# Values as one product of 129 columns per chunk, a head's output in two PSUM banks

## The chip, the cores and the metric

The kernel runs on one core of a Trainium2 chip, in one launch. A core has TensorE (matrix products, results into PSUM), VectorE, ScalarE and GpSimd (element work), and queues that start transfers. The metric is the device time of a run in microseconds, lower is better; of several runs the median counts.

## What is computed

Attention within clusters, followed by a two-level mixture of experts. The part that the change touches is the attention:

```python
q_assign = argmax(einsum('bhsd,hcd->bhsc', q_n, c_n), axis=-1)   # same for k
mask = q_assign[:, :, :, None] == k_assign[:, :, None, :]
scores = where(mask, scale * matmul(q, k.transpose(0, 1, 3, 2)), -1e9)
scores = scores - max(scores, axis=-1, keepdims=True)
attn = exp(scores)
attn = attn / (sum(attn, axis=-1, keepdims=True) + 1e-9)
x = matmul(attn, v)
```

There are 4 batches of 8 heads, 768 positions and 64 values per head, 16 clusters per head. All inputs are float32. The output of the attention, 3072 tokens of 512, goes through a router to one of 16 experts (512 to 1024 to 512 with a relu).

## The kernel before

Numbers are carried as a high part and a low part of 16 bits each, and a product of two such numbers is summed from products of parts. The 32 heads are worked off one after the other, each in nine steps. A step takes 512 of the 4608 columns that the six key chunks times 768 queries make. The order of the columns is: first all six key chunks against queries 0 to 383, then all six against queries 384 to 767. So the first half of a head's outputs is complete in the middle of its fifth step, the second at the end of the ninth.

A step (the loop at the end of `attention`) issues the following. `fine` makes the 512 scores on TensorE (L421, L422, each split in two or more products, `psf`), ScalarE takes the exponential (L426, `p`), and GpSimd subtracts the high part to leave the low part (L428, `pl`; in the last two heads VectorE does five of nine). `coarse`, up to 18 steps ahead, makes coarse scores (L379, `psc`), and VectorE takes row maxima of them (L382, `mpart`). `av` works on the step that was issued five steps before (`LAG`): it multiplies the probabilities of four blocks of 128 queries with the values, which lie in SBUF with the low parts in columns 0 to 63, the high parts in 64 to 127 and a constant in 128. For each block there are four products: high and low part of the probabilities, times high values with the constant (65 columns) and low values (64 columns), all added into the same columns of one bank of PSUM (`pso`, two banks in turn, one per head):

```python
vh, vl = vt[:, h % 2, c, 64:129], vt[:, h % 2, c, 0:64]
...
nc.tensor.matmul(out=O[:, col:col + 65], lhsT=p[:, bs], rhs=vh, ...)   # L447
nc.tensor.matmul(out=O[:, col:col + 64], lhsT=p[:, bs], rhs=vl, ...)   # L448
```

`finish` closes a head. VectorE adds a small number to the sum of the probabilities and scales it (L461), takes the reciprocal (L463) and multiplies the outputs by it in PSUM (L466). ScalarE casts the result to its high part (L467), VectorE subtracts to get the low part (L468); both go to `xs`, from which the router's logits are made (transposes L765, `logits`). `DEN` is kept: at the end `detect` looks for sums that are nearly zero.

Beside a step run the jobs of later heads: splitting inputs into parts (ScalarE L223, VectorE L224; at the start GpSimd L209, L210), the assignment to clusters (L268 to L280), the mask (L336 to L344), and routing of finished batches (L890 among it). The order of each engine's instructions is set by a scheduler that plans the whole program ahead; each engine then works its own list strictly in order, waiting where an operand is not there yet. The experts (products L1236, L1258, L1272) follow after the attention; a few of their preparations lie in it.

Of the kernel before, what the change touches and what calls it, by code (L numbers as in the profile page):

```python
# [22 lines left out]
P = 128  # L23
# [11 lines left out]
def attention(ctx, tc, qT, kT, vr, cen, R, DEN, cfg):  # L35
# [10 lines left out]
    OW = 66  # L46
# [13 lines left out]
    sp = ctx.enter_context(tc.tile_pool(name="sp", bufs=2))  # L60
    pp = ctx.enter_context(tc.tile_pool(name="pp", bufs=LAG + 2))
    sm = ctx.enter_context(tc.tile_pool(name="sm", bufs=3))
    ps_c = ctx.enter_context(tc.tile_pool(name="ps_c", bufs=2, space=PSUM))
# [8 lines left out]
    KBs, QBs, XSt, Ph, Pl, Os, mparts = {}, {}, {}, {}, {}, {}, {}  # L72
# [66 lines left out]
    nc.gpsimd.memset(obias[64:65 + C], 0.0)  # L139
    CH = const.tile([P, NP, 2, C], F16, name="CH")  # L140
# [111 lines left out]
    def assign(p, psum=None):  # L252

        pr, j = p % NP, p % 2
        if p < 2:
            ohs = [ozs[p][:, t, :, :, 64:64 + C].rearrange("p h c x -> p c h x") for t in range(2)]
        else:
            if j == 0:
                st["oh", p // 2] = sp.tile([P, NCH, P], F16, name="oh")
            ohs = [st["oh", p // 2][:, :, 64 * t + 32 * j:64 * t + 32 * j + 32].rearrange("p c (h x) -> p c h x", h=2) for t in range(2)]  # L260
# [71 lines left out]
    def mask(Q):  # L332
        oh = st["oh", Q]
        tp = ps_m.tile([P, 512], F32, name="psm").bitcast(F16)
        for c in range(NCH):
            nc.tensor.transpose(out=tp[:, c * P:(c + 1) * P], in_=oh[:, c], identity=ident)  # L336
        yield
        mk = sp.tile([P, S], F16, name="mk")
        nc.scalar.activation(out=mk, in_=tp[:, :S], func=AF.Identity, scale=mscale, bias=mbias)
        ready.add(Q)  # L340
        for i in range(4):
            h = 4 * Q + i
            nc.sync.dma_start(out=QA[h % 8][64:64 + C], in_=mk[C * i:C * i + C])
            last["mk"] = nc.sync.dma_start(out=KA[h % 8][64:64 + C], in_=mk[64 + C * i:64 + C * i + C])  # L344
# [88 lines left out]
    def av(h, u):  # L433
# [4 lines left out]
        if u == 0:  # L438
            Os[h] = ps_o.tile([P, 512], F32, name="pso")
        O = Os[h]  # L440
        for (c, q0, q1) in fsegs(u):
            vh, vl = vt[:, h % 2, c, 64:129], vt[:, h % 2, c, 0:64]
            for q in range(q0 // P, q1 // P):
                bs = slice(off, off + P)
                col = q * OW
                for i, p in enumerate((ph, pl)):
                    nc.tensor.matmul(out=O[:, col:col + 65], lhsT=p[:, bs], rhs=vh, start=c == 0 and q == 0 and i == 0, stop=False, skip_group_check=True)  # L447
                    nc.tensor.matmul(out=O[:, col:col + 64], lhsT=p[:, bs], rhs=vl, start=False, stop=c == NCH - 1 and i == 1, skip_group_check=True)  # L448
                off += P
        if u == 8:  # L450
            finish(h)

    def finish(h):

        O = Os.pop(h)
# [3 lines left out]
        Ov = O[:, 0:NCH * OW].rearrange("p (c w) -> p c w", w=OW)  # L459
        den = DEN[:, h]  # L460
        nc.vector.tensor_scalar(out=den, in0=Ov[:, :, 64], scalar1=EPS, scalar2=1.0 / XS, op0=ALU.add, op1=ALU.mult)  # L461
        rec = sm.tile([P, NCH], F32, name="rec")
        nc.vector.reciprocal(out=rec, in_=den)  # L463
        xs = XSt[b][:, :, :, hh * D:(hh + 1) * D]
        x = Ov[:, :, 0:64]
        nc.vector.tensor_tensor(out=x, in0=x, in1=rec.broadcast_to([P, NCH, D]), op=ALU.mult)  # L466
        nc.scalar.copy(out=xs[:, :, 0], in_=x)  # L467
        nc.vector.tensor_tensor(out=xs[:, :, 1], in0=x, in1=xs[:, :, 0], op=ALU.subtract)  # L468
# [82 lines left out]
    with tc.issue_after(hi0.ins), tc.issue_after(sub0.ins):  # L551
# [3 lines left out]
        for i in range(4):  # L555
            nc.gpsimd.memset(V[i][:, :, :, 128:130], SQ)
# [975 lines left out]
class Fixup:  # L1532
# [12 lines left out]
    def detect(self):  # L1545
        nc = self.nc
        EPS = 1e-9 * math.exp(PSHIFT / math.sqrt(self.vr.shape[5])) * SQ
        nc.vector.tensor_scalar(out=self.Z, in0=self.DEN, scalar1=4.0 * EPS / XS, scalar2=None, op0=ALU.is_lt)
# [150 lines left out]
```

## Time and profile before

| | us |
|---|---|
| median of 3 runs (lowest, highest) | 742.06 (740.55, 742.85) |
| the profiled execution | 742.52 |
| its span, first to last instruction | 740.7 |
| TensorE busy | 720.3 (97%) |
| VectorE busy | 596.1 (80%) |
| ScalarE busy | 486.0 (66%) |
| GpSimd busy | 493.6 (67%) |

The profile is of one execution. In its names PE is TensorE, DVE VectorE, ACT ScalarE, POOL GpSimd, and L447 is line 447 of the kernel. "out<-in" names the tile written and the tiles read. "Idle before <- X" is time that an engine stood still before an instruction, with what ended it. A record of TensorE ends when its result is written, and the next one starts long before; so starts tell its pace, and lengths do not. Records of the other engines overlap by some tens of ns in the same way. The granted clock of TensorE is full (2.4 GHz) in every stretch of the attention.

### The profile page before, as it was taken

What the parts mean: (1) busy time and instruction counts of PE and PEld (TensorE: products, weight loads), DVE (VectorE), ACT (ScalarE), POOL (GpSimd) and SP (SyncE); (2) the same over time, 40 slices, a digit from 0 to 9 for tenths busy, and PEclk for the clock granted to TensorE, in tenths of its full rate; (3) what the DMA queues carried; (4) which work ended last, traced back from release to release, by engine and by line L of the source; (5) the groups of instructions that cost most, each with busy time, mean ns of one, the idle gap of its engine ahead of it and who ended that gap; (6) DMA issues with size and microseconds to landing.
All of it is one profiled execution on the core that took longest, in us unless ns stands there. A gap on an engine that the chain in (4) does not pass through costs nothing.

```text
span 740.7 us, 26722 instructions
## 1 busy us (share of the span) xinstructions
PE 720.3 (97%) x11106; PEld 619.1 (84%) x11106; DVE 596.1 (80%) x1216; ACT 486.0 (66%) x952; POOL 493.6 (67%) x491
## 2 busy tenths in 40 slices
PE   8899999999999999999999989999999999999996
PEld 4688788888888888888888677888789999999996
DVE  6899889899888997989876476767779889988961
ACT  7778877788778887677977275444454555555642
POOL 8899787777787877878786325354644688554542
PEclk9999999999999999999999999999999999999998
DMA  8955634435245351240521696866777678887921
GB/s 226 224 141 153 192 100 119 155 99 154 81 120 172 95 159 37 67 131 3 178 81 38 234 313 220 273 211 221 237 244 234 230 272 284 284 275 264 281 77 36
DMA packets 45881, 128.04 MB, mean 173 GB/s; under 512 B 7699, under 2 KB 12691, under 8 KB 45752
## 3 DMA queue, kind: packets, MB, share of 16 engines
q1 hardware_dynamic: 40668, 112.64, 49.8%
q0 software_dynamic: 4928, 13.59, 5.1%
q8 instruction: 89, 1.46, 0.8%
q14 instruction: 40, 0.33, 0.1%
q10 hardware_dynamic: 156, 0.03, 0.0%
HBM read 93.41 MB, written 13.65 MB: 145 GB/s over the span
## 4 chain that ended last, share of the span: by engine, by line
PE 67%; DVE 17%; ACT 6%; issue 5%; DMA 2%; POOL 1%; another core or an unknown queue 1%; POOLq 0%; ACTq 0%; DVEq 0%
PE psh L1236 16%; PE psy L1258 12%; DVE mpart L382 7%; PE pso L447 6%; PE psf L421 6%; PE pso L448 5%; PE psf L422 5%; PE psc L379 5%; PE psy L1272 3%; DVE parts L224 2%; ACT p L426 2%; DMA st<-w 2%; PE psm L765 2%; PE psm L1294 1%; PE psm L1208 1%
## 5 line engine op out<-in xcount | busy, mean ns | idle before, releaser
L428 POOL TENSOR_TENSOR pl<-p 128x512 f16<-128x512 f32 x278 | 285.4, 1042 | 75.1 <-ACT p L426 70.6
L382 DVE TENSOR_REDUCE mpart<-psc 128x1 f32<-128x512 f32 (+1 forms) x282 | 190.2, 682 | 28.8 <-PE psc L379 28.4
L426 ACT ACTIVATE p<-psf 128x512 f32<-128x512 f32 x288 | 169.7, 596 | 45.6 <-PE psf L422 40.4
L447 PE MATMUL pso<-V,p 128*128 128x65 f16 x1152 | 160.2, 193 | 0.0
L448 PE MATMUL pso<-V,pl 128*128 128x64 f16 x1152 | 159.9, 193 | 0.0
L447 PE MATMUL pso<-V,pl 128*128 128x65 f16 x1152 | 159.4, 193 | 0.5 <-POOL pl L428 0.5
L448 PE MATMUL pso<-V,p 128*128 128x64 f16 x1152 | 159.3, 193 | 0.0
L421 PE MATMUL psf<-A 82*128 82x384 f16 (+2 forms) x576 | 142.5, 273 | 1.7 <-ACT p L426 1.6
L422 PE MATMUL psf<-B 128*128 128x384 f16 (+2 forms) x576 | 142.7, 273 | 0.0
L448 PEld LDWEIGHTS <-p 128*128 128x128 bf16 x1152 | 112.2, 97 | 22.2
L447 PEld LDWEIGHTS <-p 128*128 128x128 bf16 x1152 | 113.1, 98 | 9.6 <-issue 1.6
L447 PEld LDWEIGHTS <-pl 128*128 128x128 f16 x1152 | 112.5, 98 | 0.6 <-POOL pl L428 0.6
L448 PEld LDWEIGHTS <-pl 128*128 128x128 f16 x1152 | 111.5, 97 | 0.3
L379 PE MATMUL psc<-A 80*128 80x512 f16 (+1 forms) x376 | 106.3, 325 | 1.9 <-DVE mpart L382 1.2
L1239 DVE SCALAR_TENSOR_TENSOR hl<-psh,hh 128x160 f16<-128x160 f32 (+14 forms) x136 | 49.8, 368 | 48.9 <-ACT hh L1238 43.5
L1238 ACT ACTIVATE hh<-psh 128x160 f16<-128x160 f32 (+14 forms) x136 | 45.8, 345 | 59.1 <-PE psh L1236 54.9
L1301 POOL DMA_INDIRECT out_dram<-y,ri x33 | 43.4, 1316 | 52.4 <-ACT y L1300 46.3
L1236 PE MATMUL psh<-xT,wh0a 128*128 128x288 f16 (+7 forms) x512 | 74.6, 255 | 0.0
L1193 POOL DMA_INDIRECT xg<-xbuf,ri x25 | 40.5, 1620 | 43.7 <-PE psm L1208 30.1
L422 PEld LDWEIGHTS <-B 128*128 128x128 f16 x576 | 56.5, 98 | 10.9 <-issue 2.3
L1236 PE MATMUL psh<-xT,wh0b 128*128 128x272 f16 (+6 forms) x448 | 64.7, 253 | 0.0
L1236 PE MATMUL psh<-xT,wl0a 128*128 128x288 f16 (+7 forms) x256 | 64.0, 255 | 0.0
(385 smaller groups left out, 1785.9 us busy)
## 6 DMA issues: line engine op xcount, KB each, us to landing
st<-w SPq DMA_DIRECT2D x128, 512.0 KB
B<-parts SPq DMA_DIRECT2D x60, 192.0 KB
kx<-kT SPq DMA_DIRECT2D x16, 384.0 KB
qx<-qT SPq DMA_DIRECT2D x16, 384.0 KB
vx<-vr SPq DMA_DIRECT2D x16, 384.0 KB
xbuf<-xs SPq DMA_DIRECT2D x4, 1536.0 KB
A<-parts SPq DMA_DIRECT2D x30, 192.0 KB
A<-mk SPq DMA_DIRECT2D x56, 24.0 KB
```

What stands on the lines that cost most here:

```text
L379: last["mm"] = nc.tensor.matmul(out=pc[:, off:off + k1 - k0], lhsT=QA[h % 8][0:80, c * P:(c + 1) * P], rhs=KA[h % 8][0:80, k0:k1], start=T ...
L382: nc.vector.tensor_reduce(out=(mp[:, 0, 0:1], mp[:, :, 1], mp[:, 1, 0:1])[i], in_=pc.rearrange("p (a x) -> p a x", a=n), axis=AX.X, op=ALU ...
L421: nc.tensor.matmul(out=o, lhsT=KA[h % 8][0:82, ks], rhs=QA[h % 8][0:82, q0:q1], start=True, stop=False)
L422: nc.tensor.matmul(out=o, lhsT=KBs[h][:, ks], rhs=QBs[h][:, q0:q1], start=False, stop=True)
L426: cfg["exp"] = nc.scalar.activation(out=p32, in_=pf, func=AF.Exp, scale=QK / (SQ * SQ))
L428: lo = (nc.vector if u in (EARLY if h < 2 else DVE_LO[h % 8] if h < NH - 2 else DVE_END) else nc.gpsimd).tensor_tensor(out=pl, in0=p32, in ...
L447: nc.tensor.matmul(out=O[:, col:col + 65], lhsT=p[:, bs], rhs=vh, start=c == 0 and q == 0 and i == 0, stop=False, skip_group_check=True)
L448: nc.tensor.matmul(out=O[:, col:col + 64], lhsT=p[:, bs], rhs=vl, start=False, stop=c == NCH - 1 and i == 1, skip_group_check=True)
L1236: self.mm = nc.tensor.matmul(out=ph[:, 0:M], lhsT=w[:, k, fs], rhs=xT[:, a, k], start=i == 0, stop=i == 3 * KD - 1)
L1238: nc.scalar.activation(out=hh[:, f], in_=ph[:, 0:M], func=AF.Relu)
L1239: self.ev = nc.vector.scalar_tensor_tensor(out=hl[:, f], in0=ph[:, 0:M], scalar=0.0, in1=hh[:, f], op0=ALU.max, op1=ALU.subtract)
L1258: self.mm = nc.tensor.matmul(out=py[:, 0:M], lhsT=w[:, f, d * P:(d + 1) * P], rhs=a[:, f], start=i == 0, stop=i == len(prods) - 1)
```

## The change

The two products with the parts of the values become one of 129 columns (0 to 128 of the value tile), whose low half and high half land in separate columns of PSUM. A block of queries needs 130 columns, so a bank holds three blocks, and a head takes two banks, one for each half of its queries. A new function `joined` is called when a half is complete: ScalarE copies the low halves to SBUF (`ol`), VectorE adds them to the high halves and writes the sum to SBUF (`xo`, one buffer). The constant column and a constant in `ol` now carry the scale and the small number of the denominator, so that the reciprocal is taken directly and kept in `DEN`; `detect` compares the other way round. The multiply works in SBUF, and the low part of the outputs is made by GpSimd, in the last two heads by VectorE. To make room, two tiles (`oh`, `mk`) get one buffer in place of two.

```diff
--- before.py
+++ after.py
@@ -43,7 +43,8 @@
     PS = math.exp(QK * PSHIFT)
     EPS = 1e-9 * PS * SQ
     VW = 136
-    OW = 66
+    OW = 130
+    HB = NCH // 2
     NQ = B * H // 4
     NH = B * H
     LAG = 5
@@ -58,8 +59,10 @@
     ring = ctx.enter_context(tc.tile_pool(name="ring", bufs=8))
     ld = ctx.enter_context(tc.tile_pool(name="ld", bufs=2))
     sp = ctx.enter_context(tc.tile_pool(name="sp", bufs=2))
+    sq1 = ctx.enter_context(tc.tile_pool(name="sq1", bufs=1))
     pp = ctx.enter_context(tc.tile_pool(name="pp", bufs=LAG + 2))
     sm = ctx.enter_context(tc.tile_pool(name="sm", bufs=3))
+    xo = ctx.enter_context(tc.tile_pool(name="xo", bufs=1))
     ps_c = ctx.enter_context(tc.tile_pool(name="ps_c", bufs=2, space=PSUM))
     ps_f = ctx.enter_context(tc.tile_pool(name="ps_f", bufs=2, space=PSUM))
     ps_o = ctx.enter_context(tc.tile_pool(name="ps_o", bufs=2, space=PSUM))
@@ -69,7 +72,7 @@
     ident = cfg["ident"]
 
     cparts, ready, last = {}, set(), {}
-    KBs, QBs, XSt, Ph, Pl, Os, mparts = {}, {}, {}, {}, {}, {}, {}
+    KBs, QBs, XSt, Ph, Pl, Os, Xs = {}, {}, {}, {}, {}, {}, {}
 
 
     st = {}
@@ -137,6 +140,7 @@
     obias = const.tile([P, 1], F32, name="obias")
     nc.gpsimd.memset(obias[64:96], PSHIFT)
     nc.gpsimd.memset(obias[64:65 + C], 0.0)
+    OL = [const.tile([P, HB, 65], F32, name=f"ol{i}") for i in range(2)]
     CH = const.tile([P, NP, 2, C], F16, name="CH")
     CL = const.tile([P, NP, 2, C], F16, name="CL")
     nc.vector.memset(CH, 0.0)
@@ -256,7 +260,7 @@
             ohs = [ozs[p][:, t, :, :, 64:64 + C].rearrange("p h c x -> p c h x") for t in range(2)]
         else:
             if j == 0:
-                st["oh", p // 2] = sp.tile([P, NCH, P], F16, name="oh")
+                st["oh", p // 2] = sq1.tile([P, NCH, P], F16, name="oh")
             ohs = [st["oh", p // 2][:, :, 64 * t + 32 * j:64 * t + 32 * j + 32].rearrange("p c (h x) -> p c h x", h=2) for t in range(2)]
         simt = psum or ps_m.tile([P, 512], F32, name="psm")
         sim = simt[:, 0:NCH * 4 * C].rearrange("p (c t x) -> p c t x", c=NCH, t=2)
@@ -335,7 +339,7 @@
         for c in range(NCH):
             nc.tensor.transpose(out=tp[:, c * P:(c + 1) * P], in_=oh[:, c], identity=ident)
         yield
-        mk = sp.tile([P, S], F16, name="mk")
+        mk = sq1.tile([P, S], F16, name="mk")
         nc.scalar.activation(out=mk, in_=tp[:, :S], func=AF.Identity, scale=mscale, bias=mbias)
         ready.add(Q)
         for i in range(4):
@@ -435,37 +439,42 @@
         vt = V[(h // 2) % 4]
         off = 0
         ph, pl = Ph.pop((h, u)), Pl.pop((h, u))
-        if u == 0:
-            Os[h] = ps_o.tile([P, 512], F32, name="pso")
-        O = Os[h]
         for (c, q0, q1) in fsegs(u):
-            vh, vl = vt[:, h % 2, c, 64:129], vt[:, h % 2, c, 0:64]
+            vv = vt[:, h % 2, c, 0:129]
             for q in range(q0 // P, q1 // P):
+                if c == 0 and q % HB == 0:
+                    Os[h] = ps_o.tile([P, 512], F32, name="pso")
                 bs = slice(off, off + P)
-                col = q * OW
+                o = Os[h][:, q % HB * OW:q % HB * OW + 129]
                 for i, p in enumerate((ph, pl)):
-                    nc.tensor.matmul(out=O[:, col:col + 65], lhsT=p[:, bs], rhs=vh, start=c == 0 and q == 0 and i == 0, stop=False, skip_group_check=True)
-                    nc.tensor.matmul(out=O[:, col:col + 64], lhsT=p[:, bs], rhs=vl, start=False, stop=c == NCH - 1 and i == 1, skip_group_check=True)
+                    nc.tensor.matmul(out=o, lhsT=p[:, bs], rhs=vv, start=c == 0 and q % HB == 0 and i == 0, stop=c == NCH - 1 and i == 1, skip_group_check=True)
                 off += P
+                if c == NCH - 1 and q % HB == HB - 1:
+                    joined(h, q // HB)
         if u == 8:
             finish(h)
 
+    def joined(h, i):
+
+        Ov = Os.pop(h)[:, 0:HB * OW].rearrange("p (c w) -> p c w", w=OW)
+        ol = OL[i]
+        nc.scalar.copy(out=ol[:, :, 0:64], in_=Ov[:, :, 0:64])
+        if i == 0:
+            Xs[h] = xo.tile([P, NCH, 65], F32, name="xo")
+        nc.vector.tensor_tensor(out=Xs[h][:, HB * i:HB * (i + 1)], in0=Ov[:, :, 64:129], in1=ol, op=ALU.add)
+
     def finish(h):
 
-        O = Os.pop(h)
+        X = Xs.pop(h)
         b, hh = h // H, h % H
         if hh == 0:
             XSt[b] = xsp.tile([P, NCH, 2, H * D], F16, name="xs")
-        Ov = O[:, 0:NCH * OW].rearrange("p (c w) -> p c w", w=OW)
-        den = DEN[:, h]
-        nc.vector.tensor_scalar(out=den, in0=Ov[:, :, 64], scalar1=EPS, scalar2=1.0 / XS, op0=ALU.add, op1=ALU.mult)
-        rec = sm.tile([P, NCH], F32, name="rec")
-        nc.vector.reciprocal(out=rec, in_=den)
+        nc.vector.reciprocal(out=DEN[:, h], in_=X[:, :, 64])
         xs = XSt[b][:, :, :, hh * D:(hh + 1) * D]
-        x = Ov[:, :, 0:64]
-        nc.vector.tensor_tensor(out=x, in0=x, in1=rec.broadcast_to([P, NCH, D]), op=ALU.mult)
+        x = X[:, :, 0:64]
+        nc.vector.tensor_tensor(out=x, in0=x, in1=DEN[:, h].broadcast_to([P, NCH, D]), op=ALU.mult)
         nc.scalar.copy(out=xs[:, :, 0], in_=x)
-        nc.vector.tensor_tensor(out=xs[:, :, 1], in0=x, in1=xs[:, :, 0], op=ALU.subtract)
+        (nc.gpsimd if h < NH - 2 else nc.vector).tensor_tensor(out=xs[:, :, 1], in0=x, in1=xs[:, :, 0], op=ALU.subtract)
 
 
 
@@ -553,7 +562,9 @@
         split(1, 0, True)
         splitv(0, True)
         for i in range(4):
-            nc.gpsimd.memset(V[i][:, :, :, 128:130], SQ)
+            nc.gpsimd.memset(V[i][:, :, :, 128:130], SQ / XS)
+        for t in OL:
+            nc.gpsimd.memset(t[:, :, 64], EPS / XS)
     with tc.issue_after(last["qa"].ins), tc.issue_after(last["sub"].ins):
         split(2, 1, True)
     banks = itertools.cycle(((ps_c, "psc"), (ps_f, "psf")))
@@ -1545,7 +1556,7 @@
     def detect(self):
         nc = self.nc
         EPS = 1e-9 * math.exp(PSHIFT / math.sqrt(self.vr.shape[5])) * SQ
-        nc.vector.tensor_scalar(out=self.Z, in0=self.DEN, scalar1=4.0 * EPS / XS, scalar2=None, op0=ALU.is_lt)
+        nc.vector.tensor_scalar(out=self.Z, in0=self.DEN, scalar1=XS / (4.0 * EPS), scalar2=None, op0=ALU.is_gt)
         nc.vector.tensor_reduce(out=self.zs, in_=self.Z, axis=AX.XY, op=ALU.max)
         nc.vector.tensor_copy(out=self.zh, in_=self.zs)
         yield
```

The numbers of the lines behind the change are shifted by four to eleven. What stands where in the engines' lists is shown at three places: TensorE in head 16, VectorE and ScalarE at the end of head 11 (heads counted from 0).

TensorE, at the start of a step's value products before (`psc` coarse scores, `p` and `pl` parts of the probabilities, `V` values, `pso` outputs):

```order
L379 LDWEIGHTS A_187
L379 MATMUL psc<-A_187 128x512
L447 LDWEIGHTS p_6258
L447 MATMUL pso<-V_192,p_6258 128x65
L448 LDWEIGHTS p_6258
L448 MATMUL pso<-V_192,p_6258 128x64
L447 LDWEIGHTS pl
L447 MATMUL pso<-V_192,pl 128x65
L448 LDWEIGHTS pl
L448 MATMUL pso<-V_192,pl 128x64
```

And the same place now:

```order
L383 LDWEIGHTS A_193
L383 MATMUL psc<-A_193 128x256
L450 LDWEIGHTS p_5172
L450 MATMUL pso<-V_198,p_5172 128x129
L450 LDWEIGHTS pl
L450 MATMUL pso<-V_198,pl 128x129
```

Four weight loads and four products per block of queries have become two and two; the block that follows repeats the pattern.

VectorE before, at the end of head 11 (`DEN`, `rec`: denominator and reciprocal; `mx`, `psm`, `mw`, `oh`: assignment; `xs`: outputs in parts):

```order
L382 TENSOR_REDUCE mpart_220<-psc 128x2
L461 TENSOR_SCALAR DEN<-pso 128x6
L275 TENSOR_TENSOR psm<-psm,mx 128x384
L463 RECIPROCAL rec<-DEN 128x6
L382 TENSOR_REDUCE mpart_220<-psc 128x1
L466 TENSOR_TENSOR pso<-pso,rec 128x6x64
L276 TENSOR_TENSOR psm<-psm,desc 128x384
L382 TENSOR_REDUCE mpart_220<-psc 128x1
L468 TENSOR_TENSOR xs<-pso,xs 128x6x64
L278 TENSOR_REDUCE mw<-psm 128x24
```

And now (`ol`, `xo`: low halves and joined outputs):

```order
L386 TENSOR_REDUCE mpart_228<-psc 128x2
L464 TENSOR_TENSOR xo<-pso,ol_221 128x195
L277 TENSOR_REDUCE mx<-psm 128x24
L472 RECIPROCAL DEN<-xo 128x6
L386 TENSOR_REDUCE mpart_228<-psc 128x1
L475 TENSOR_TENSOR xo<-xo,DEN 128x6x64
L279 TENSOR_TENSOR psm<-psm,mx 128x384
L228 TENSOR_TENSOR V_198<-psm,V_198 128x6x64
L280 TENSOR_TENSOR psm<-psm,desc 128x384
```

The denominator step has become the sum of a half, the multiply has one other instruction between it and the reciprocal as before, and the subtraction to `xs` is gone from this list; it stands in GpSimd's list between two low parts of the probabilities.

ScalarE before, at the same head (`psm<-vx` and `V`: splitting of values):

```order
L426 ACTIVATE p_4828<-psf 128x512
L249 ACTIVATE V_193<-vx 128x12x64
L426 ACTIVATE p_4875<-psf 128x512
L223 ACTIVATE psm<-vx 128x384
L426 ACTIVATE p_4907<-psf 128x512
L467 CAST xs<-pso 128x6x64
L426 ACTIVATE p_4939<-psf 128x512
```

And now:

```order
L430 ACTIVATE p_4030<-psf 128x512
L461 COPY ol_221<-pso 128x3x64
L227 ACTIVATE psm<-vx 128x384
L430 ACTIVATE p_4069<-psf 128x512
L253 ACTIVATE V_199<-vx 128x12x64
L430 ACTIVATE p_4093<-psf 128x512
L476 CAST xs<-xo 128x6x64
L430 ACTIVATE p_4117<-psf 128x512
```

The copy of the second half is put in five instructions ahead of the cast, with two exponentials between them.

## Rows read from the trace of the kernel before

**Rows 1.** Page, first part: busy us (share of the span) and instructions.

```profile
PE 720.3 (97%) x11106; PEld 619.1 (84%) x11106; DVE 596.1 (80%) x1216; ACT 486.0 (66%) x952; POOL 493.6 (67%) x491
```

**Rows 2.** Timeline, one attention step, TensorE: start us, length us, line, operation, shapes.

```profile
100.38 0.20 PE L447 MATMUL pso<-V,p 128*128 128x65 f16 x1
...
100.86 0.22 PE L421 MATMUL psf<-A 82*128 82x128 f16 x1
100.92 0.22 PE L422 MATMUL psf<-B 128*128 128x128 f16 x1
100.98 0.33 PE L421 MATMUL psf<-A 82*128 82x384 f16 x1
...
101.53 0.19 PE L447 MATMUL pso<-V,p 128*128 128x65 f16 x1
```

**Rows 3.** Waits of TensorE, whole span: total us, times, longest us.

```profile
PE psf L421 <- ACT p L426: 1.6, 5, 0.7
PE psc L379 <- DVE mpart L382: 1.2, 3, 0.4
PE pso L447 <- POOL pl L428: 0.5, 1, 0.5
```

**Rows 4.** Stretches: window, us; PE, PEld, DVE, ACT, POOL busy (instructions); clock, DMA share, GB/s.

```profile
76.00:88.00 12.00, 11.95 (x239) 10.03 (x236) 12.00 (x27) 10.67 (x21) 10.21 (x14) 1.00 0.73 215
88.00:100.00 12.00, 11.27 (x216) 9.26 (x215) 7.49 (x19) 8.84 (x18) 8.43 (x25) 1.00 0.27 73
...
160.00:172.00 12.00, 11.70 (x233) 9.62 (x230) 11.84 (x27) 9.15 (x21) 9.55 (x10) 1.00 0.55 154
...
256.00:268.00 12.00, 11.81 (x262) 9.97 (x260) 11.83 (x27) 9.01 (x20) 9.73 (x10) 1.00 0.60 176
...
sum 372.00, PE 366.97 PEld 308.02 DVE 320.50 ACT 290.11 POOL 292.61; mean PE 11.84 PEld 9.94 DVE 10.34 ACT 9.36 POOL 9.44
```

**Rows 5.** Chain that ended last, in time: start us, us, what.

```profile
397.44 0.33 PE psm L765 x6
...
448.43 1.47 PE psh L1236 x12
```

**Rows 6.** Timeline of TensorE in the experts' stage, the shape of L1236.

```profile
448.51 0.29 PE L1236 MATMUL psh<-xT,wl0a 128*128 128x288 f16 x1
```

**Rows 7.** VectorE's groups, 60 to 400: busy us, mean ns, idle before.

```profile
L468 DVE TENSOR_TENSOR xs<-pso,xs 128x384 f16<-128x384 f32 x29 | 16.0, 553 | 3.4 <-ACT xs L467 3.1
...
L280 DVE TENSOR_TENSOR oh<-psm,mw 128x192 f16<-128x192 f32 x24 | 7.3, 348 | 0.0
...
L890 DVE TENSOR_TENSOR rmv<-oe,rmv 128x384 f16<-128x384 f16 x3 | 2.7, 913 | 0.0
```

**Rows 8.** Timeline of VectorE after the last head's products.

```profile
402.25 0.17 DVE L461 TENSOR_SCALAR DEN<-pso 128x6 f32<-128x6 f32 x1 [0.27 <-PE pso L448]
```

**Rows 9.** VectorE's groups, 400 to the end.

```profile
L823 DVE TENSOR_TENSOR rmv<-oe,rmv 128x384 f16<-128x384 f16 x1 | 0.5, 547 | 0.0
```

**Rows 10.** Line 428 on VectorE: ns min/median/max, first and last start.

```profile
L428 DVE TENSOR_TENSOR pl<-p x10: 680/693/1356, 381.9 to 399.1; 128x512 f16<-128x512 f32 x10
```

**Rows 11.** Timelines of GpSimd and of VectorE, 388.5 to 392.

```profile
389.55 1.05 POOL L428 TENSOR_TENSOR pl<-p 128x512 f16<-128x512 f32 x1
...
389.80 1.96 DVE L428 TENSOR_TENSOR pl<-p 128x512 f16<-128x512 f32 x2
```

**Rows 12.** ScalarE's groups, 60 to 400.

```profile
L426 ACT ACTIVATE p<-psf 128x512 f32<-128x512 f32 x262 | 154.5, 596 | 40.7 <-PE psf L422 35.6 <-POOL pl L428 2.1 <-PE psc L379 2.1
...
L223 ACT ACTIVATE psm<-qx 128x384 f32<-128x384 f32 x24 | 11.7, 487 | 2.1 <-DVE parts L224 2.0
...
L406 ACT COPY mr<-psm 6x128 f16<-6x128 f16 x28 | 7.0, 248 | 0.8 <-PE psm L403 0.3
```

**Rows 13.** GpSimd's groups, 40 to 410.

```profile
L428 POOL TENSOR_TENSOR pl<-p 128x512 f16<-128x512 f32 x269 | 276.3, 1043 | 72.6 <-ACT p L426 68.3 <-ACT roh L857 0.5
```

**Rows 14.** Line 210: ns min/median/max, first and last start, forms.

```profile
L210 POOL TENSOR_TENSOR parts<-qx,parts x3: 914/1639/1642, 7.8 to 30.9; 128x768 f16<-128x768 f32 x2, 128x384 f16<-128x384 f32 x1
```

## The prediction

> **What bounds the kernel now.** I read the page's busy line first: TensorE is busy for 97% of the span [rows 1]. The ends of its records are modelled, so that share alone proves nothing. The next view is therefore the starts of its instructions inside one step of attention [rows 2]. The reader is to see that every start follows the one before at the pace of the columns: sixteen value products between 100.38 and 100.86, then the fine scores, the coarse scores, and the next step's products at 101.53, with no hole. A bare step takes 101.53 - 100.38 = 1.15 us and TensorE fills it. The waits of TensorE confirm this: over the whole span it waited 1.6 us for ScalarE's exponentials, 1.2 us for VectorE's row maxima and 0.5 us for GpSimd's low parts [rows 3]. So in attention TensorE sets the pace, and time that it saves is time saved, as long as the others can follow.
>
> Whether they can is in the table by stretches of 12 us [rows 4]. The 31 stretches from 40 to 412 us have VectorE busy for 10.34 of 12 us on average, but unevenly: in 12 of them it is busy for 11.2 us or more (12.00 in 76:88, 11.84 in 160:172, 11.83 in 256:268), and between them it falls as low as 7.49. ScalarE (9.36) and GpSimd (9.44) have more room. VectorE is thus within a few per cent of being a second bound for some two fifths of attention, and idle for a fifth to a third of the time elsewhere. The experts' stage after about 415 us is not touched by the change and is taken to move as a whole.
>
> **The value products.** Of the four products of a chunk (65, 64, 65, 64 columns) two of 129 are left: 258 columns before, 258 after. A step of 16 products becomes one of 8, so what goes is not columns but whatever each product costs beside them. The sixteen took 0.48 us, 30.0 ns each [rows 2]; 64.5 columns at 2.4 GHz are 26.9 ns, so a product costs 3.1 ns on its own account. Longer ones show the same: twelve of 288 columns take 1.47 us, 122.5 ns each, 2.5 above the 120 of the columns; six transposes of 128 take 0.33 us, 55 ns each, 1.7 above [rows 5, 6]. Saved are 8 x 3.1 = 25 ns in each of 288 steps, 7.2 us. Bounds: with a remainder of 2.5 ns a product of 129 takes 56.3 ns, eight take 450 ns, and 30 x 288 = 8.6 us are saved. The other end is the pair of fine products of 128 columns, which follow at 60 ns each (100.86, 100.92, 100.98) [rows 2]: 60.4 ns for 129, eight make 483 ns, a loss of 0.9 us. The value products are nearer to the first kind in weights (all 128 rows; one of the fine pair has 82), so I take 7.2. Half of the weight loads go too; I cost them at nothing, since the starts above already run at the pace of the columns.
>
> **VectorE.** Per head go the shifted denominator (L461, 0.17 us) and the low part (L468, 553 ns), together 0.72 us [rows 7, 8]; two joining sums of 195 elements come, which I price by the nearest row, 348 ns for 192 elements [rows 7], together 0.70 us. In work that is nothing. The multiply by the reciprocal stays, but both of its inputs now lie in SBUF, where the values were in PSUM before. What this costs beside GpSimd the trace shows in two places. The same 384-element product of two SBUF inputs takes 547 ns in the tail (L823), with GpSimd idle, and 913 ns on average in its three calls in attention (L890) [rows 7, 9]. And VectorE's own low parts (L428), 680 ns at best, take up to 1356 [rows 10]: the timeline has GpSimd's low part from 389.55 to 390.60, and a VectorE low part issued at 389.80, in a pair that takes 1.96 us where two at their best end within 2 x 0.68 = 1.36 [rows 11]. The added time is what was left of GpSimd's instruction. So 32 multiplies gain 913 - 547 = 0.37 us each, 11.7 us on VectorE in all; at worst a whole GpSimd instruction of 1.04 us, at best nothing. Queued behind the multiply on VectorE are the coarse row maxima, and TensorE waits for these with two banks in hand; behind it on ScalarE is the cast that waits for the multiply, then the next exponential.
> The Trainium skill says so too (SBUF — State Buffer, section "Who interferes with whom"): a VectorE instruction with two SBUF inputs and a GpSimd instruction that reads SBUF exclude one another for a whole instruction, and whichever came first is finished first. By that rule, the trace agrees (the 1356 and 913 ns above), every multiply can be caught, and the worst sum is that of the slower rival below.
> How much of the 11.7 us reaches TensorE depends on the stretch. In the 19 lighter stretches VectorE has 1 us or more to spare and I take nothing. In the 12 heavy ones (12/31 of 32 heads, 12.4 heads) there are 12.4 x 0.37 = 4.5 us; two banks of coarse scores and the instruction that stands between reciprocal and multiply hide part of it, and I take half, 2.3 us. In the same stretches a faster TensorE runs into VectorE: of the 2.8 us saved there (12.4/32 of 7.2) I take half as not realised, 1.4 us.
>
> **ScalarE.** 64 copies of 192 elements come. Between 248 ns for 128 elements and 487 ns for 384 [rows 12] I take 310 ns, 20 us in all, 0.6 us per head of about 11.7 us. Cover: in attention it sat idle for 40.7 us before its exponentials, 35.6 of them waiting for TensorE [rows 12]. I take nothing; were that cover gone in the four stretches where ScalarE is at 10.9 us or more, 4 x 0.6 = 2.5 us.
>
> **GpSimd.** It gets 30 of the 32 low parts of the outputs. The nearest row is 914 ns for 384 elements [rows 14]; 512 take 1043 [rows 13], which would scale to 0.78. That makes 24 to 27 us on an engine that waits 68.3 us for the exponentials [rows 13]. Its low parts are wanted five steps later, which covers a delay of one. I take nothing. The bound: nine low parts and one of these make 10.3 us, nine bare steps without 25 ns each 10.1, so a head with nothing else in it would be 0.2 us late, at most 30 x 0.2 = 6 us; most heads have more than bare steps in them.
>
> **The rest.** The one-buffer tiles are written again 36 steps later, long after their last reading. A bank of products comes back after half a head (over 5 us) and is emptied within about 1 us. After the last head the chain to the router's logits gets a copy (0.31) and a sum (0.35) for the denominator step (0.17) [rows 8]: +0.5 us.
>
> **Sum.** -7.2 + 2.3 + 1.4 + 0.5 = -3.0 us, 0.4%, against the profiled execution's 742.52 us (span 740.7, 1.8 around it): 739.5. That execution lay 0.46 above the median of 742.06, so I predict 739.0.
>
> **Rivals.**
> Slower: the exclusion of VectorE and GpSimd becomes the bound. Place: the multiply of each head; price 0.37 us each, all of it on TensorE: -7.2 + 11.7 + 0.5 = +5.0, 747.1 us. For it: VectorE at 12.00 of 12 [rows 4], the 913 ns [rows 7], and GpSimd, which is held up in turn. Against it: the light stretches. It decides from about 8.9 of the 11.7 us on, three quarters, where the result passes +2.2.
> No change: the heavy stretches take their gain back in full. -7.2 + 2.8 + 4.5 + 0.5 = +0.6, 742.7 us; the bounds of ScalarE (2.5) or GpSimd (up to 6), in part, end near here too. For it: [rows 4]. Against it: in these same stretches TensorE is still busy for 11.7 of 12 us.
> The remainder per product grows: 129 columns behave like the fine pair. +0.9 + 2.3 + 0.5 = +3.7, 745.8 us. For it: the 60 ns [rows 2]; against it: the 2.5 and 1.7 ns [rows 5, 6].
> That the change does not do what it says I leave out: the order shows one product of 129 columns where there were two.
>
> **Chances.** Forecast 0.46 (its own range 735 to 741); no change 0.31; exclusion 0.17; remainder 0.06. A difference under 0.3% (2.2 us) can't be told from none here. Faster 0.46, same 0.31, slower 0.23. The best end is 742.06 - 8.6 + 0.5 = 734.0, the worst of the cases 747.1; I give 734 to 746.5.
>
> **What the profile after would show.** Value products starting 56 to 57 ns apart (60 would speak for the remainder). The multiply averaging about 0.9 us against 0.56, spread between 0.55 and 1.5; were it at 0.56, the exclusion is wrong and the result nearer to 735. TensorE's waits for VectorE's row maxima and ScalarE's exponentials up by 2 to 4 us in all, in the heavy stretches; ten or more make the forecast wrong. The end of attention about 3 us earlier, and the experts' stage as long as before.

## The result and the profile after

The change makes the kernel slower: 745.97 us (median of 5 runs, 744.41 to 747.1) against 741.73 us (5 runs, 740.55 to 742.85) before it, ratio 1.0055 [1.0035, 1.0075]. The forecast was 739.0 us. The time lies inside the range that was given (734 to 746.5), but on the side of a loss where a gain was forecast. The profiled execution took 747.1 us, with a span of 745.1.

The page's busy line, in the columns of [rows 1]:

```profile
PE 716.5 (96%) x8802; PEld 610.7 (82%) x8802; DVE 607.3 (81%) x1218; ACT 500.6 (67%) x1016; POOL 528.0 (71%) x523
```

TensorE has 2304 instructions and 3.8 us of busy time less, in a span that is 4.4 us longer. VectorE gained 11.2 us, GpSimd 34.4, ScalarE 14.6. One bare step of attention on TensorE, as in [rows 2]:

```profile
101.91 0.22 PE L450 MATMUL pso<-V,p 128*128 128x129 f16 x1
...
102.36 0.22 PE L425 MATMUL psf<-A 82*128 82x128 f16 x1
...
103.03 0.22 PE L450 MATMUL pso<-V,p 128*128 128x129 f16 x1
```

Eight products in 0.45 us and the step in 1.12, where before sixteen took 0.48 and the step 1.15. So the saving is there in a step without a hole. Part of what took it back stands in TensorE's waits over the whole span, as in [rows 3] (total us, times, longest):

```profile
PE psc L383 <- DVE mpart L386: 5.6, 10, 1.5
PE psf L425 <- ACT p L430: 2.2, 4, 1.4
PE pso L450 <- POOL pl L432: 0.5, 1, 0.5
```

The wait for VectorE's row maxima went from 1.2 us in 3 waits to 5.6 in 10, and its longest from 0.4 to 1.5. Stretches as in [rows 4], others among them; the last line sums the 32 stretches from 40 to 424 (in [rows 4] it is 31, from 40 to 412):

```profile
64.00:76.00 12.00, 10.32 (x144) 8.28 (x142) 10.92 (x19) 10.70 (x23) 10.96 (x15) 1.00 0.53 135
76.00:88.00 12.00, 11.86 (x167) 9.87 (x165) 11.61 (x28) 10.14 (x23) 10.76 (x16) 1.00 0.67 190
88.00:100.00 12.00, 11.78 (x164) 9.60 (x162) 9.88 (x24) 11.39 (x22) 11.54 (x14) 1.00 0.34 114
100.00:112.00 12.00, 11.59 (x146) 9.44 (x144) 10.72 (x22) 9.28 (x22) 11.02 (x27) 1.00 0.52 144
...
256.00:268.00 12.00, 11.46 (x164) 9.39 (x162) 12.00 (x27) 9.90 (x23) 11.22 (x11) 1.00 0.71 190
...
sum 384.00, PE 372.10 PEld 306.25 DVE 336.24 ACT 306.49 POOL 327.37; mean PE 11.63 PEld 9.57 DVE 10.51 ACT 9.58 POOL 10.23
```

The worst stretch for TensorE is 64:76 (10.32 of 12 us busy), where VectorE is at 10.92, not one of those that were full before. The groups of VectorE, ScalarE and GpSimd from 60 to 400 us that are new or carry the argument (busy us, mean ns, idle time before):

```profile
L475 DVE TENSOR_TENSOR xo<-xo,DEN 128x384 f32<-128x384 f32 x30 | 24.4, 812 | 0.3
L464 DVE TENSOR_TENSOR xo<-pso,ol 128x195 f32<-128x195 f32 x58 | 20.6, 355 | 5.2 <-ACT ol L461 2.6 <-ACT desc L394 1.2
```

```profile
L461 ACT COPY ol<-pso 128x192 f32<-128x192 f32 x58 | 18.6, 320 | 2.3 <-PE pso L450 2.2
```

```profile
L477 POOL TENSOR_TENSOR xs<-xo,xs 128x384 f16<-128x384 f32 x29 | 26.0, 897 | 1.1 <-ACT xs L476 1.0
L432 POOL TENSOR_TENSOR pl<-p 128x512 f16<-128x512 f32 x254 | 266.2, 1067 | 41.8 <-ACT p L430 36.5 <-ACT mr L410 2.3 <-DMA A<-mk 0.3
```

Copies, sums and low parts cost what they were priced at (310, 348, and 780 to 914 ns). The multiply is the line to look at. All 32 of it by line (ns min/median/max, first and last start), before and then after:

```profile
L466 DVE TENSOR_TENSOR pso<-pso,rec x32: 552/562/567, 47.1 to 403.0; 128x384 f32<-128x384 f32 x32
```

```profile
L475 DVE TENSOR_TENSOR xo<-xo,DEN x32: 546/584/2543, 48.3 to 406.8; 128x384 f32<-128x384 f32 x32
```

Half of them are about as quick as before; the mean of 812 comes from the others, the longest of which is over four times as long. The longest, on VectorE, on GpSimd, and on TensorE (start us, length us; in brackets the idle time ahead and its releaser):

```profile
70.59 0.65 DVE L386 TENSOR_REDUCE mpart<-psc 128x1 f32<-128x512 f32 x1
71.16 2.54 DVE L475 TENSOR_TENSOR xo<-xo,DEN 128x384 f32<-128x384 f32 x1
73.63 0.54 DVE L277 TENSOR_REDUCE mx<-psm 128x24 f32<-128x384 f32 x1
74.09 0.54 DVE L228 TENSOR_TENSOR parts<-psm,parts 128x384 f16<-128x384 f32 x1
74.56 0.67 DVE L386 TENSOR_REDUCE mpart<-psc 128x2 f32<-128x512 f32 x1
```

```profile
70.26 3.03 POOL L432 TENSOR_TENSOR pl<-p 128x512 f16<-128x512 f32 x3
```

```profile
73.60 0.22 PE L450 MATMUL pso<-V,pl 128*128 128x129 f16 x1
75.29 0.38 PE L383 MATMUL psc<-A 80*128 80x512 f16 x1 [1.47 <-DVE mpart L386]
```

The multiply stands on VectorE from 71.16 to 73.70, while GpSimd works off three low parts in a row from 70.26 to 73.29; the multiply ends 0.41 us after the last of them. Between two row maxima (70.59 and 74.56) VectorE thus lets 4 us pass. The next product on TensorE's list is one of coarse scores, which wants a bank that these maxima empty, and after the value product of 73.60 it starts only at 75.29. A multiply of 1.3 us is enough for a small hole, in the stretch 100:112 with VectorE busy for 10.72 of 12 us (VectorE, then TensorE):

```profile
108.23 1.32 DVE L475 TENSOR_TENSOR xo<-xo,DEN 128x384 f32<-128x384 f32 x1
109.47 1.28 DVE L386 TENSOR_REDUCE mpart<-psc 128x1 f32<-128x512 f32 x2
```

```profile
109.46 0.33 PE L426 MATMUL psf<-B 128*128 128x384 f16 x1
110.20 0.38 PE L383 MATMUL psc<-A 80*128 80x512 f16 x1 [0.41 <-DVE mpart L386]
```

For a number that holds all such places I took the starts of TensorE's instructions from 40 to 410 us, and of every distance what exceeds the columns at 2.4 GHz plus 2.5 ns, where that is over 15 ns (a product of fewer than 64 columns is counted as one of 64). These holes sum to 10.7 us before and 20.5 us after.

### The profile page after: what moved, and what is told of

It is laid out like the page before. It is cut to its first block, busy times and chain, and to the rows that moved or that the text cites. A ratio compares the mean times of both kernels' runs of the same rounds, so it can differ in the third digit from the quotient of the medians.

```text
span 745.1 us, 22241 instructions
## 1 busy us (share of the span) xinstructions
PE 716.5 (96%) x8802; PEld 610.7 (82%) x8802; DVE 607.3 (81%) x1218; ACT 500.6 (67%) x1016; POOL 528.0 (71%) x523
## 4 chain that ended last, share of the span: by engine, by line
PE 62%; DVE 11%; ACT 9%; DMA 7%; issue 6%; POOL 4%; SPq 0%; POOLq 0%; ACTq 0%; DVEq 0%
PE psh L1247 16%; PE psy L1269 14%; PE pso L450 9%; PE psf L425 5%; PE psf L426 4%; PE psc L383 4%; DVE mpart L386 3%; PE psy L1283 3%; ACT p L430 3%; DMA kx<-kT 3%; DMA st<-w 2%; POOL pl L432 2%; PE psm L1305 2%; DVE parts L228 1%; PE psm L1219 1%
## 5 line engine op out<-in xcount | busy, mean ns | idle before, releaser
L432 POOL TENSOR_TENSOR pl<-p 128x512 f16<-128x512 f32 x278 | 291.2, 1066 | 47.6 <-ACT p L430 42.1
L450 PE MATMUL pso<-V,p 128*128 128x129 f16 x1152 | 164.4, 220 | 0.0
L450 PE MATMUL pso<-V,pl 128*128 128x129 f16 x1152 | 163.2, 219 | 0.5 <-POOL pl L432 0.5
L450 PEld LDWEIGHTS <-pl 128*128 128x128 f16 x1152 | 112.2, 97 | 20.4 <-POOL pl L432 0.9
L450 PEld LDWEIGHTS <-p 128*128 128x128 bf16 x1152 | 112.1, 97 | 13.2 <-issue 5.6
L1312 POOL DMA_INDIRECT out_dram<-y,ri x33 | 41.2, 1250 | 50.3 <-ACT y L1311 45.0
L425 PEld LDWEIGHTS <-A 82*128 82x128 f16 x576 | 56.2, 98 | 12.4 <-issue 2.7
L1247 PE MATMUL psh<-xT,wl0b 128*128 128x272 f16 (+6 forms) x224 | 55.9, 253 | 0.0
L1247 PEld LDWEIGHTS <-wh0a 128*128 128x128 f16 x512 | 46.7, 98 | 4.7
L1033 DVE SCALAR_TENSOR_TENSOR wl1b<-st,wh1b 128x1024 f16<-128x1024 f32 x32 | 47.0, 1469 | 0.4 <-POOL wh1b L1032 0.4
```

Source lines behind the costliest of these rows:

```text
L425: nc.tensor.matmul(out=o, lhsT=KA[h % 8][0:82, ks], rhs=QA[h % 8][0:82, q0:q1], start=True, stop=False)
L432: lo = (nc.vector if u in (EARLY if h < 2 else DVE_LO[h % 8] if h < NH - 2 else DVE_END) else nc.gpsimd).tensor_tensor(out=pl, in0=p32, in ...
L450: nc.tensor.matmul(out=o, lhsT=p[:, bs], rhs=vv, start=c == 0 and q % HB == 0 and i == 0, stop=c == NCH - 1 and i == 1, skip_group_check=True)
L1033: nc.vector.scalar_tensor_tensor(out=l, in0=st, scalar=WS, in1=h, op0=ALU.mult, op1=ALU.subtract)
L1247: self.mm = nc.tensor.matmul(out=ph[:, 0:M], lhsT=w[:, k, fs], rhs=xT[:, a, k], start=i == 0, stop=i == 3 * KD - 1)
```

## Experiments

Ratios are against the kernel before on the same chip; its medians were 743.15 us (e1 to e4), 738.98 (e5 to e8) and 738.68 (e9, e10). Edits are to the changed kernel, those of e6 and e7 to the kernel before. "Holes" is the sum just defined.

**e1: multiply from PSUM.** The joined half goes back into its bank, and each half is multiplied from there.

```diff
-        nc.vector.tensor_tensor(out=Xs[h][:, HB * i:HB * (i + 1)], in0=Ov[:, :, 64:129], in1=ol, op=ALU.add)
+        nc.vector.tensor_tensor(out=Ov[:, :, 64:129], in0=Ov[:, :, 64:129], in1=ol, op=ALU.add)
+        den = DEN[:, h, HB * i:HB * (i + 1)]
+        nc.vector.reciprocal(out=den, in_=Ov[:, :, 128])
+        nc.vector.tensor_tensor(out=Xs[h][:, HB * i:HB * (i + 1), 0:64], in0=Ov[:, :, 64:128], in1=den.broadcast_to([P, HB, D]), op=ALU.mult)
     def finish(h):
-        nc.vector.reciprocal(out=DEN[:, h], in_=X[:, :, 64])
-        nc.vector.tensor_tensor(out=x, in0=x, in1=DEN[:, h].broadcast_to([P, NCH, D]), op=ALU.mult)
```

> The joining sum is written back into PSUM, the reciprocal and the multiply follow for each half at once, the multiply reads PSUM and writes SBUF; so VectorE's multiply has one SBUF input. ScalarE's copies and GpSimd's low parts of the outputs stay. Theory A (VectorE's multiply and GpSimd exclude one another, and the blocked multiply delays the row maxima that TensorE waits for): no multiply above 0.4 us, TensorE's waits for the row maxima fall from 5.6 to 1 to 2 us, 735 to 738 us. Theory B (the 64 copies on ScalarE delay the exponentials) or C (GpSimd's 30 added low parts): no better than the changed kernel, 744 to 747 us.

Measured: 738.93 us, ratio 0.9932 [0.9916, 0.9947], faster than both kernels, though 0.9 us above the range of theory A. Its multiplies by line, and TensorE's wait for the row maxima:

```profile
L467 DVE TENSOR_TENSOR xo<-pso,DEN x64: 339/348/361, 42.0 to 401.0; 128x192 f32<-128x192 f32 x64
```

```profile
PE psc L383 <- DVE mpart L386: 0.4, 1, 0.4
```

No multiply is longer than 361 ns, though VectorE has one more reciprocal and one more multiply per head. The holes are 14.8 us. ScalarE's copies and GpSimd's low parts are all still there, so neither is what makes the changed kernel slower than the one before. Changed with the inputs are the halving and the places in the order, so e5 takes these alone.

**e2: outputs' low parts on VectorE.**

```diff
-        (nc.gpsimd if h < NH - 2 else nc.vector).tensor_tensor(out=xs[:, :, 1], in0=x, in1=xs[:, :, 0], op=ALU.subtract)
+        nc.vector.tensor_tensor(out=xs[:, :, 1], in0=x, in1=xs[:, :, 0], op=ALU.subtract)
```

> The changed kernel with the low parts of the outputs made by VectorE in all heads (two SBUF inputs, 384 elements). Theory A: 30 more instructions that can be blocked, 0.7 to 0.9 us each instead of 0.55, and 0.46 us more work for VectorE: 748 to 754 us. Theory C: GpSimd is relieved of 26 us, 740 to 744 us. Theory B: 745 to 748 us.

Measured: 750.49 us, ratio 1.0094 [1.0074, 1.0114]; holes 24.8 us.

```profile
L475 DVE TENSOR_TENSOR xo<-xo,DEN x32: 546/1000/1412, 46.9 to 410.1; 128x384 f32<-128x384 f32 x32
```

A second instruction per head with two SBUF inputs makes it worse (the low parts themselves average 855 ns, against 553 from PSUM in [rows 7]). Taking these parts off VectorE was not the harm.

**e3: the wider products alone.** Joining is left out, and with it the low halves of the values in the result; each half is finished from PSUM, its low part on VectorE.

```diff
-        nc.scalar.copy(out=ol[:, :, 0:64], in_=Ov[:, :, 0:64])
-        nc.vector.tensor_tensor(out=Xs[h][:, HB * i:HB * (i + 1)], in0=Ov[:, :, 64:129], in1=ol, op=ALU.add)
+        nc.vector.reciprocal(out=den, in_=Ov[:, :, 128])
+        x = Ov[:, :, 64:128]
+        nc.vector.tensor_tensor(out=x, in0=x, in1=den.broadcast_to([P, HB, D]), op=ALU.mult)
...
+        nc.vector.tensor_tensor(out=xs[:, :, 1], in0=x, in1=xs[:, :, 0], op=ALU.subtract)
```

> Only the products: 129 columns and two banks, but no joining (the low halves are left out of the result), and each half is finished in PSUM as the kernel before did it, the low parts by VectorE with one SBUF input. No copies on ScalarE, nothing added on GpSimd. If the products gain what their starts say (6 to 7 us): 734 to 737 us under all theories. If the gain of the products is itself not there: 740 to 743 us.

Measured: 737.55 us, ratio 0.9916 [0.9897, 0.9935]; holes 13.6 us. The products are a gain when nothing is joined: 743.15 - 737.55 = 5.6 us. The interval reaches from 4.8 to 7.7, so the time alone does not tell this from the whole 7 us; the holes, 2.9 us above before, speak for less.

**e4: without ScalarE's copies** (the low halves are left out; the tile that the sum adds holds zeros).

```diff
-        nc.scalar.copy(out=ol[:, :, 0:64], in_=Ov[:, :, 0:64])
+            nc.gpsimd.memset(t[:, :, 0:64], 0.0)
```

> The changed kernel without ScalarE's 64 copies (the low halves are left out; VectorE adds a constant tile). Multiply in SBUF and GpSimd's low parts stay. Theory B: 738 to 741 us. Theory A or C: 743 to 746 us, multiplies still up to 1.3 us and more.

Measured: 748.79 us, ratio 1.0062 [1.004, 1.0083]; holes 24.2 us.

```profile
L474 DVE TENSOR_TENSOR xo<-xo,DEN x32: 546/916/3528, 46.9 to 406.3; 128x384 f32<-128x384 f32 x32
```

ScalarE has 64 instructions less and the kernel is no faster; it lies above what either theory expected. It isn't a clean removal, since the multiplies fell at other moments of GpSimd's work and became longer (mean 960 ns). It excludes the copies as the main cause, no more.

**e5: e1's halves, but the sum stays in SBUF.**

```diff
         nc.vector.tensor_tensor(out=Xs[h][:, HB * i:HB * (i + 1)], in0=Ov[:, :, 64:129], in1=ol, op=ALU.add)
+        X = Xs[h][:, HB * i:HB * (i + 1)]
+        den = DEN[:, h, HB * i:HB * (i + 1)]
+        nc.vector.reciprocal(out=den, in_=X[:, :, 64])
+        nc.vector.tensor_tensor(out=X[:, :, 0:64], in0=X[:, :, 0:64], in1=den.broadcast_to([P, HB, D]), op=ALU.mult)
```

> The changed kernel with reciprocal and multiply for each half at once, as in the version with the sum in PSUM, but the sum stays in SBUF, so the two multiplies of 192 elements have two SBUF inputs each. It parts what helped there. Theory A (exclusion): multiplies average 0.5 us or more against 0.35, some over 1 us, 744 to 750 us on a chip where the kernel before takes about 743. Theory E (finishing by halves spreads the work, and that is what helped): 738 to 740 us.

Measured: 744.85 us, ratio 1.0069 [1.0043, 1.0096]; holes 23.2 us.

```profile
L468 DVE TENSOR_TENSOR xo<-xo,DEN x64: 339/543/2668, 40.8 to 408.3; 128x192 f32<-128x192 f32 x64
```

```profile
PE psf L425 <- ACT p L430: 4.8, 12, 1.3
PE psc L383 <- DVE mpart L386: 2.3, 8, 0.5
```

The same instructions as in e1, 349 ns on average there and 695 here. The halves did not help e1; the input in PSUM did.

**e6 and e7: one more product per head, before.** Into a tile that the low part overwrites; `EX` is a constant in SBUF, `x` lies in PSUM. First e6, then e7:

```diff
+        nc.vector.tensor_tensor(out=xs[:, :, 1], in0=EX.broadcast_to([P, NCH, D]), in1=rec.broadcast_to([P, NCH, D]), op=ALU.mult)
```
```diff
+        nc.vector.tensor_tensor(out=xs[:, :, 1], in0=x, in1=rec.broadcast_to([P, NCH, D]), op=ALU.mult)
```

> The kernel before with one more product of 384 elements per head on VectorE, right behind the multiply, two SBUF inputs (a constant and the reciprocals); its output is overwritten by the low part. Theory A: the added product averages about 0.9 us, single ones up to 1.5 and more; against the kernel with the same added product reading PSUM 4 to 10 us slower.

> The kernel before with one more product of 384 elements per head on VectorE, in the same place, one input from PSUM and one from SBUF. Only the work of 0.46 us per head is added: 0.56 us each, without long ones, 1 to 5 us slower than the kernel before.

Measured: e6 751.79 us, 1.0166 [1.014, 1.0192], holes 21.3; e7 744.09 us, 1.0065 [1.0042, 1.0088], holes 13.1. The extra product by line and TensorE's wait for the row maxima, two rows of e6, then the same two of e7:

```profile
L469 DVE TENSOR_TENSOR xs<-ex,rec x32: 545/987/1415, 47.4 to 415.2; 128x384 f16<-128x384 f32 x32
```

```profile
PE psc L381 <- DVE mpart L384: 8.4, 13, 1.1
```

```profile
L469 DVE TENSOR_TENSOR xs<-pso,rec x32: 542/548/558, 48.1 to 406.3; 128x384 f16<-128x384 f32 x32
```

```profile
PE psc L381 <- DVE mpart L384: 2.9, 9, 0.4
```

This comes nearest to the price alone. (The scheduler also placed some of the other instructions anew: 57 of VectorE's 1249 stand in another order in e7 than in e6.) Both inputs in SBUF make the product 0.40 us longer on average (950 against 550 ns), 12.8 us in 32, and the kernel 751.79 - 744.09 = 7.7 us, from the two intervals give or take about 2.6: some 60% arrives at the end. Plain work arrives less: a product of e7 moves VectorE's list on by about 0.46 us (it takes 0.55, and the next instruction overlaps its end, as at 73.63 and 74.09 above), 14.7 us in 32, and these cost 744.09 - 738.98 = 5.1 us, a third.

**e8: the changed kernel again, no edit.**

> The changed kernel itself, on the chip of the other three, as their base: 1.0035 to 1.0075 times the kernel before.

Measured: 741.73 us, ratio 1.0032 [1.0016, 1.0049]: slower again, a little less than expected, on a chip on which both kernels are 3 to 4 us quicker than in the first comparison. Its multiplies:

```profile
L475 DVE TENSOR_TENSOR xo<-xo,DEN x32: 546/582/2546, 47.0 to 405.2; 128x384 f32<-128x384 f32 x32
```

The same multiplies are blocked, for times that differ by some ns (the long one starts at 69.8 and takes 2546 ns), and the holes sum to 20.5 us as in the first trace. So the holes belong to the kernel and not to one execution.

**e9: e3 with the joining,** copy and sum in PSUM as in e1, cast and low part per half from PSUM, the low part on VectorE.

```diff
+        nc.vector.tensor_tensor(out=Ov[:, :, 64:129], in0=Ov[:, :, 64:129], in1=ol, op=ALU.add)
+        nc.vector.reciprocal(out=den, in_=Ov[:, :, 128])
+        nc.vector.tensor_tensor(out=x, in0=x, in1=den.broadcast_to([P, HB, D]), op=ALU.mult)
+        nc.scalar.copy(out=xs[:, :, 0], in_=x)
+        nc.vector.tensor_tensor(out=xs[:, :, 1], in0=x, in1=xs[:, :, 0], op=ALU.subtract)
```

> All of the change but GpSimd's part: 129 columns, two banks, joining by ScalarE and VectorE with the sum in PSUM, and reciprocal, multiply, cast and low part for each half in PSUM, the low part by VectorE with one SBUF input. Nothing is excluded by GpSimd, VectorE has 0.5 us per head more to do than with the low part on GpSimd. If VectorE's plain work counts as in the kernel with the extra product from PSUM (5 us for 15 us of work): 0.9965 to 1.000 of the kernel before, 3 to 5 us slower than the sum in PSUM with GpSimd's low parts.

**e10: e1 again.**

> The version with the sum and the multiply in PSUM and the low parts on GpSimd, again on the chip of the other, as its base: 0.9916 to 0.9947 of the kernel before.

Measured: e9 739.24 us, 1.0006 [0.9994, 1.0018], holes 17.5; e10 736.54 us, 0.9964 [0.9951, 0.9978], holes 14.9. Both lie above what was expected, and e10 is 2.7 us quicker than e9 where 3 to 5 were expected. TensorE's wait for the row maxima, in e9 and in e10:

```profile
PE psc L383 <- DVE mpart L386: 3.1, 10, 0.5
```

```profile
PE psc L383 <- DVE mpart L386: 0.4, 1, 0.4
```

In e9 no instruction that makes the outputs has two SBUF inputs (VectorE's low parts of the probabilities in the last two heads still have, the longest 1519 ns), yet VectorE has all the work and the gain is used up. With the low parts of the outputs on GpSimd (e10) 2.7 us of it are back. That speaks for the change's move to GpSimd, but does not show it alone: e9 also casts by halves. How large e1's gain is stays open: 0.9932 and 0.9964, each measured against the kernel before on its own chip, have intervals that do not overlap.

## Why the prediction was wrong, point by point

**TensorE as the bound, and the products: right.** Without the holes, starts of value products in after are 56.9 ns apart on average (a p product to the pl product behind it) and 56.3 (pl to p), 113.2 per block of two, against 119.6 per block of four before: 6.4 x 1152 = 7.4 us, forecast 7.2. The rival of a growing remainder (60 ns) falls.

**ScalarE, GpSimd and VectorE's plain work: the prices right, ScalarE's cover not.** The durations are above. GpSimd's wait for the exponentials before its low parts fell from 68.3 us [rows 13] to 38.7 in the same stretch from 40 to 410 us, so it took its new work into that time. For ScalarE the prediction took nothing, on the ground of its idle time; what the traces show of that stands below.

**The price of a multiply: right in kind, too high in size.** Forecast 0.37 us each, 11.7 in all; measured 0.812 - 0.561 = 0.25, 8.0 in all. It is no steady surcharge: the median rose by 22 ns, the longest by 2 us, more than the "at worst a whole GpSimd instruction of 1.04 us" that was put as the bound. (The pair of rows that this was read from, [rows 11], shows 0.60 us more where 0.80 were left of GpSimd's instruction.)

**What of it reaches TensorE: this step failed.** The prediction said "In the 19 lighter stretches VectorE has 1 us or more to spare and I take nothing", and half in the heavy ones. But the spare time of 12 us says nothing on a delay of 1 or 2 us in one place. TensorE is covered by two banks of coarse scores, and a single blocked multiply outlasts these however idle VectorE is later: the holes at 74 and at 110 us lie in stretches that before were among the 19 lighter ones:

```profile
64.00:76.00 12.00, 11.22 (x229) 9.33 (x227) 10.94 (x25) 10.27 (x23) 10.06 (x15) 1.00 0.66 163
100.00:112.00 12.00, 12.00 (x223) 9.92 (x222) 9.79 (x20) 8.71 (x19) 10.88 (x12) 1.00 0.52 147
```

With the change VectorE is busy there for 10.9 and 10.7 of 12 us. (Nor was it idle for "a fifth to a third of the time" in all the lighter ones: in seven of the 19 it was busy for 10.4 to 11.0.) The holes grew by 20.5 - 10.7 = 9.8 us where the forecast had 2.3 + 1.4 = 3.7, which turns -7.4 into +2.4. That agrees with the time from the first value product to the last, which grew by 2.5 us (376.7 before, 379.3 after). From there to the end of the last multiply it is 0.5 us more, as forecast. The rest of the span's +4.4, a later start (0.8) and what follows the last multiply (0.6), is no more than two traces of one kernel differ by: the first exponential starts at 25.0 us in after and at 23.7 in e8.

A part of the 9.8 has nothing to do with the blocked multiplies. In e1, with all multiplies at full speed, the holes are still 4.1 us above before. Sorted by the engine whose instruction ended them, as the releasers in the traces have it (us):

| holes ended by | before | after | e1 | e3 |
|---|---|---|---|---|
| VectorE | 7.7 | 10.6 | 4.7 | 3.5 |
| ScalarE | 2.5 | 8.3 | 9.1 | 8.4 |
| others | 0.5 | 1.6 | 1.0 | 1.7 |

So with the multiplies free VectorE holds TensorE up less than before, and ScalarE about 6 us more, for which the prediction had put nothing. One such place, from 40 to 410 us: TensorE's weight loads for the transpose of a head's row maxima wait for ScalarE's cast of these, in after, e1 and e3, and in before no such wait stands:

```profile
PEld L407 <- ACT desc L394: 3.2, 9, 0.5
PEld L407 <- ACT desc L394: 2.7, 8, 0.7
PEld L406 <- ACT desc L393: 3.7, 9, 0.5
```

The copies are not its cause, since e3 has none; what is stays open, as the order of all lists is new in each version. The 1.4 us that I took for a faster TensorE running into VectorE are thus not what e1 shows. The other 5.7 us (20.5 - 14.8) go with the multiply's input, the term I set at 2.3, and nearly all of them are holes that VectorE ended (10.6 against 4.7). The split is worked out from traces that e8 and e10 repeat (holes of 20.5 and 14.9). Not every long hole starts at a multiply: the second longest in after, 1.6 us at 391, has a low part of the probabilities on VectorE at its root, which stood for 3.13 us. The multiply of that head, ScalarE's cast and the next exponentials all came late by it:

```profile
386.18 3.73 DVE L432 TENSOR_TENSOR pl<-p 128x512 f16<-128x512 f32 x2
392.84 0.32 PE L425 MATMUL psf<-A 82*128 82x384 f16 x1 [1.39 <-ACT p L430]
```

What is shown by times is that with an input in PSUM the kernel is faster than before (e1, e10), with the same halves in SBUF slower (e5), and that this input is worth 7.7 us in the kernel before (e6, e7), in each pair but for the order of some instructions. The sign that the prediction gave did not tell the failure: TensorE's waits for row maxima and exponentials rose by 5.0 us in all (1.2 and 1.6 before, 5.6 and 2.2 after), between the "2 to 4" that it expected and the "ten" that were to make it wrong.

So it was the rival "the exclusion of VectorE and GpSimd becomes the bound", with 747.1 us against 745.97 measured, though not by its own sum: the multiplies lost 8.0 us instead of 11.7, of which by the split above 5.7 reached TensorE instead of all, and the 4.1 us of other holes, which the rival left out, made up most of the difference. That its time came so near is luck in part.

The Trainium skill (SBUF — State Buffer, section "Who interferes with whom") lets a VectorE instruction with at most one SBUF input, outside the 2-port modes, run beside GpSimd, and has one with two exclude GpSimd instructions that read SBUF. The traces agree: on average 349 ns in e1 against 695 in e5, 550 in e7 against 950 in e6. It also says that the order of issue decides who is blocked. The multiply at 71.16, which by the records stood first against the low parts that began at about 71.3 and 72.3, ended only after both. By that rule it should have waited for one; the measurement decides.

## What to carry to other kernels

Beside a busy GpSimd, keep one input of a VectorE product in PSUM: with the sum in SBUF rather than back in its bank, a gain of 0.4 to 0.7% was here a loss of 0.3 to 0.7%. Price an instruction that can be blocked by its longest delay against the buffers of whoever waits behind it, not by its mean against a stretch's idle time. And do not count a saving on the engine that sets the pace as whole: of 7.4 us here 2 (e10) to 6 (e3) arrived even in the best versions, and ScalarE, whose mean idle time looked ample, ended most of the holes that were left there (9.1 of 14.8 us in e1).

## What the runs showed of the hardware that was not expected

A blocked VectorE instruction does not always get the next turn: the 546-ns multiply stood 2.54 us and let two whole GpSimd low parts of about 1.01 us pass, and one in e4 stood 3.53 us. The same happens to VectorE's own low parts of the probabilities in the changed kernel, whose longest was 1356 ns before [rows 10]:

```profile
L432 DVE TENSOR_TENSOR pl<-p x10: 676/686/3131, 384.2 to 402.7; 128x512 f16<-128x512 f32 x10
```

Chips differ more than the effect studied: the same kernel before had medians of 743.15, 738.98 and 738.68 us on the three of e1 to e10. A comparison of two kernels across chips, as of e1 with e5, is therefore one of ratios, and even these agree only to about 0.3% (e1 and e10).
